# Sums of an attention kernel by DMA transpose in 116 units instead of 96, and its last unit in two halves

## The chip, the cores and the metric

The kernel runs on one core of one Trainium2 chip. A core has TensorE (PE, matrix products; its weight loads are listed as PEld), VectorE (DVE), ScalarE (ACT), GpSimd (POOL) and SyncE (SP, which here only issues transfers). Each works through its own list of instructions in order; semaphores tie the lists together. The metric is the device time of one execution in microseconds.

## The reference

B = 1, 2048 tokens, width D = 512, 32 heads of 128, 2048 cached keys, inputs in bfloat16:

```python
x = A_x
xn = _layernorm(x)
q = (xn @ wq).reshape(B, Sq, 32, 128).transpose(0, 2, 1, 3)
scores = einsum("bhqd,bhkd->bhqk", q, k_cache) * 128 ** -0.5
o = einsum("bhqk,bhkd->bhqd", softmax(scores), v_cache)
s = o.transpose(0, 2, 1, 3).reshape(B, Sq, 4096) @ wo
h = _gelu(_layernorm(xn) @ w1)                # four column groups shifted by 1, -1, 2, -2 tokens
x1 = xn + shifted(h) @ w2
g = _silu(x1 + _gelu(_layernorm(x1) @ w3) @ w4)   # w3: 512 x 1792
return x + s * g
```

## The kernel before, in words

All instructions stay in the order in which the program names them: `pin` keeps them so on each engine, and `mm` (L109) issues every matmul. The tile framework adds the semaphores.

A prologue computes the layernorms and the MLP. `m1` to `m4` are its four products, `x1` and `x2` add a product to `xall`, `stats` and `ln2` make the second layernorm. The second half of the last product (tiles 8 to 15, `m4`) is left over: `held_mm` slips it into the first units of the attention loop. `q_ahead` makes the queries of some units during the prologue.

The attention is a loop over 128 **units**: 8 groups of 4 heads, in each group 4 query blocks of 512 tokens, in each block the 4 heads. A unit has 8 **slots** (`SPU`), and `n` counts slots over all units. In a slot, `s_slot` makes the scores of 256 keys by two matmuls of 512 columns into a pair of PSUM banks (`psS`, two pairs), and ACT takes their exponentials into a quarter of `pT` (L291). `pv_run` follows `lag` slots later with `pv_slot`: two matmuls of values by exponentials into `ps_o` (`psO`, two banks). The lag is 5 at first, 10 from unit 12, and 5 again at the end.

The softmax sums take two ways. DVE always adds the four `pT` quarters to one 128 x 512 tile `acc` (L297, L302, then L307 and L308). In units outside `TURN`, `sums` multiplies this by a column of ones on TensorE: four matmuls of one column into a bank of `psX` with the tag `xa`, which the query projection `q_mm` uses as well; DVE takes the reciprocals (L327). In units inside `TURN` (12 to 107), `turn` transposes `acc` by a DMA on SP's queue (L333), and `turned_sums` sums it on DVE (L338) and takes the reciprocals (L340). Both write the reciprocals to DRAM (`dr`), and `bcast` (L346) reads them back to all partitions as `rb`. `norm` (L358) multiplies `ps_o` by `rb` into `oT`, which frees the bank of `ps_o`. In turned units the token order of `rb` differs from that of `ps_o`: `rb` is read in steps of 4 elements (16 bytes), `ps_o` and `oT` in a row.

When all four heads of a block are normalised, `wo_mm` multiplies `oT` by their rows of wo, one tile of 128 tokens after another, and `wo_post` adds the product to `sacc` (L399, L411, or L404 and L407 for late tiles). In the last group it also gates and writes out (L420, L422, or `y_out` L392). SP's queue carries, in order, the loads of K (transposed), V, wq and wo pieces of the next group, `turn`'s transposes, `dr`, `rb` and the outputs.

The last two units are called UA (126) and UB (127). UB has no round trip through DRAM for its sums: `late_sums` sums by matmuls with a column of twos, and the reciprocals scale the rows of its part of the product (`late_wo`, `last_act`, L458), which an identity matmul (`join`) adds to the part of the other three heads (`last_wo`).

Of the kernel before, what the change touches and what calls it, by code (L numbers as in the profile page):

```python
# [17 lines left out]
def kernel(  # L18
# [62 lines left out]
    ident = const.tile([P, P], BF16, name="ident")  # L81
    diag = const.tile([P, P], FP32, name="diag")
# [36 lines left out]

    units = [(g, qt, hh) for g in range(NG) for qt in range(QT) for hh in range(HG)]  # L120
# [3 lines left out]
    TURN = range(3 * HG, NU - 5 * HG)  # L124
    PV0, PV1 = 2 * HG, NU - 5 * HG + 3
# [177 lines left out]

    def add_last(u):
        add_next(u, 3)
        a = st[u]["acc"]
        pin(nc.vector.tensor_tensor(out=a[:, 0:2, :], in0=a[:, 0:2, :], in1=a[:, 2:4, :], op=ALU.add))  # L307
        pin(nc.vector.tensor_tensor(out=a[:, 0, :], in0=a[:, 0, :], in1=a[:, 1, :], op=ALU.add))  # L308
# [11 lines left out]
    def sums(u):  # L320
        s = st[u]
        ps = psX.tile([P, 4], FP32, tag="xa", name="ps_sum")
        a = s["acc"][:, 0, :].rearrange("k (p j) -> k j p", j=4)
        for j in range(4):
            mm(ps[:, j:j + 1], a[:, j, :], ones_t[:], True, True)
        rc = smp.tile([P, 4], FP32, name="rc")
        pin(nc.vector.reciprocal(out=rc[:], in_=ps[:]))  # L327
# [21 lines left out]
    def norm(u):  # L349
# [17 lines left out]
    def wo_mm(g, t, hhs):  # L367
        if hhs[0] == 0:
            wo_box[0] = psX.tile([P, D], FP32, tag="xm", name="ps_wo")
        oT = oTs[(g, t // 4)]  # L370
        ts = t % 4
        for hh in hhs:
            mm(wo_box[0][:], oT[:, hh, ts * P:(ts + 1) * P], wos[g * HG + hh][:], hh == 0, hh == HG - 1)
# [53 lines left out]
    def late_sums(u, src, first, last):  # L427
        if first:
            st[u]["sum"] = psX.tile([P, 4], FP32, tag="xa", name="ps_sum")
        ps = st[u]["sum"]  # L430
        for j in range(4):
            for i, a in enumerate(src):
                mm(ps[:, j:j + 1], a[:, j * P:(j + 1) * P], twos_t[:],
                   first and j == 0 and i == 0, last and j == 3 and i == len(src) - 1)

    def late_rc(u):
        rc = smp.tile([P, 4], FP32, tag="rl", bufs=2, name="rl")
        pin(nc.vector.reciprocal(out=rc[:], in_=st[u]["sum"][:]))
        st[u]["rc"] = rc

    def late_o(u):
        s = st[u]
        s["ou"] = pB.tile([P, 512], BF16, tag="ou", bufs=1, name="ou")
        for c in (slice(0, 256), slice(256, 512)):
            pin(nc.scalar.activation(out=s["ou"][:, c], in_=s["o"][:, c], func=ACT.Identity))

    def late_wo(u, ts, ps):
        h = units[u][0] * HG + units[u][2]
        mm(ps, st[u]["ou"][:, ts * P:(ts + 1) * P], wos[h][:], True, True)

    def last_wo(ts, ps, hhs=(0, 1, 2), stop=False):
        for hh in hhs:
            mm(ps, oTs[(NG - 1, QT - 1)][:, hh, ts * P:(ts + 1) * P], wos[(NG - 1) * HG + hh][:],
# [105 lines left out]
    for u in range(NU - 4 * HG, NU - 3 * HG):  # L559
# [8 lines left out]
    for u in (2 * HG, NU - 12, NU - 2, NU - 1):  # L568
# [60 lines left out]
    HELD = 7  # L629
    heldps = {}  # L630

    def held_part(t, a, b, tag="xm"):
        if a == 0:
            heldps[t] = psX.tile([P, 512], FP32, tag=tag, name="ps_m")
        m4(t, heldps[t], range(a, b))
# [7 lines left out]
    def held_mm(n):  # L643
        u, p = divmod(n, SPU)
        if u == 0 and p < 2:
            held_part(8, 7 * p, 7 * p + 7, "xa")
            if p == 1:
                held_out(8, n)
        elif u == 0:
            held_part(9, FC * (p - 2) // 6, FC * (p - 1) // 6)  # L650
            if p == SPU - 1:
                held_out(9, n)
        elif u < HELD:
            if p < SPU - 1:
                held_part(9 + u, 2 * p, 2 * p + 2)
            if p == SPU - 2:
                held_out(9 + u, n)
# [28 lines left out]
    def wo_slot(part, n, each=2):  # L686
        gg, t = wo_todo[0]
        if part < HG // each:
            wo_mm(gg, t, tuple(range(part * each, (part + 1) * each)))
# [7 lines left out]
    for v in range(1, NU):  # L697
        if v not in made:
            for dc in range(DC):
                k = dc - 1 if v - 2 in TURN else dc // 2  # L700
                q_plan[(v - 1) * SPU + k].append((v, (dc,)))

    for n in range(UB * SPU):
        u, p = divmod(n, SPU)
        extra = len(wo_todo) > 3 and u < 2 * HG + 2 and pS is not None or u >= UA - 1
# [14 lines left out]
        if twice and p < 3:  # L720
            wo_slot(p, n)
        if p == (3 if u - 1 in TURN else 2) and u + 1 not in made:
# [133 lines left out]
```

## Time and profile before

| | us |
|---|---|
| median of 3 runs | 1253.55 (1253.39 to 1253.73) |
| the profiled execution | 1253.59 |
| its span, first to last instruction | 1251.8 |
| PE busy | 1237.9 |
| ACT busy | 1101.5 |
| DVE busy | 1031.9 |

The granted TensorE clock was 0.999 of full speed over the span. A row of a group gives line, engine, operation, what is written from what, the count, the busy time and the mean of one in ns, and then the idle time of the engine before it with what ended it. A row of the timeline gives the start, the time, and the same names; rows that follow each other are merged (x2), and then the time is that of all together. Matmuls overlap, so the time of one is longer than the distance to the next. In a row of stretches, the busy times stand in the order PE, PEld, DVE, ACT, POOL. Idle time of an engine that does not set the end costs nothing.

### The profile page before, as it was taken

How to read it: one execution, taken by the hardware profiler on the slowest of the kernel's cores; microseconds unless marked ns; L12 is line 12 of the kernel's file. 1: busy time of each engine (PE TensorE's matmuls, PEld its weight loads, DVE VectorE, ACT ScalarE, POOL GpSimd, SP SyncE). 2: the span in 40 equal slices, each digit the busy share in tenths (PEclk: the TensorE clock that was granted, in tenths of full speed). 3: DMA queues.
4: the chain of work that ended last, by engine and by line, in shares of the span. 5: the costliest groups of instructions: out<-in, count | busy, mean ns of one | idle time of the engine just before them, and what ended most of it. 6: DMA issues, size and time to landing. Idle time of an engine off the chain costs nothing.

```text
span 1251.8 us, 16270 instructions
## 1 busy us (share of the span) xinstructions
PE 1237.9 (99%) x5814; PEld 597.8 (48%) x5931; DVE 1031.9 (82%) x1430; ACT 1101.5 (88%) x1117; POOL 35.5 (3%) x91
## 2 busy tenths in 40 slices
PE   9999999999999999999999999999999999999998
PEld 4444444444444444444444444444444444444443
DVE  7621567788888988888888888888888999978888
ACT  5344888999999999999999999999999999998886
POOL 5310000000000000000000000000000000000000
PEclk9999999999999999999999999999999999999999
DMA  6482112444244523453244514353244424442222
GB/s 180 112 161 54 18 26 43 87 106 81 53 89 93 118 52 64 97 110 77 68 83 106 103 39 93 80 119 68 57 100 102 103 66 86 99 92 50 68 56 59
DMA packets 224945, 103.86 MB, mean 83 GB/s; under 512 B 176928, under 2 KB 208160, under 8 KB 224864
## 3 DMA queue, kind: packets, MB, share of 16 engines
q1 hardware_dynamic: 223488, 100.33, 37.7%
q0 software_dynamic: 672, 1.84, 0.8%
q8 instruction: 46, 0.75, 0.3%
q10 hardware_dynamic: 704, 0.66, 0.2%
q14 instruction: 35, 0.29, 0.1%
HBM read 67.90 MB, written 2.36 MB: 56 GB/s over the span
## 4 chain that ended last, share of the span: by engine, by line
PE 96%; DVE 2%; issue 1%; ACT 1%; DMA 1%; POOL 0%; SPq 0%; DVEq 0%; ACTq 0%
PE ps_s L109 39%; PE ps_o L109 36%; PE ps_q L109 9%; PE ps_wo L109 9%; PE ps_m L109 2%; DVE acc L302 0%; DMA rb<-dr 0%; PE ps_sum L109 0%; PE ps_w L109 0%; DMA xin<-in_A_x_dram 0%; ACT qT L277 0%; DVE y L392 0%; DVE xall L420 0%; ACT pT L291 0%; DVE sacc L411 0%
## 5 line engine op out<-in xcount | busy, mean ns | idle before, releaser
L291 ACT ACTIVATE pT<-ps_s 128x1024 bf16<-128x1024 f32 x1024 | 1035.2, 1024 | 75.4 <-PE ps_s L109 27.8
L109 PE MATMUL ps_s<-qT,kT 128*128 128x512 bf16 x2041 | 607.6, 379 | 0.6
L109 PE MATMUL ps_o<-pT,vb 128*128 128x512 bf16 x1962 | 588.9, 379 | 0.5
L302 DVE TENSOR_TENSOR acc<-acc,pT 128x2048 bf16<-128x2048 bf16 x255 | 309.3, 1213 | 83.7 <-ACT pT L291 80.2
L109 PEld LDWEIGHTS <-kT 128*128 128x128 bf16 x2048 | 230.3, 113 | 226.6 <-issue 0.8
L109 PEld LDWEIGHTS <-vb 128*128 128x128 bf16 x2048 | 200.3, 98 | 226.4 <-issue 0.4
L109 PE MATMUL ps_wo<-wo_h,oT 128*128 128x512 bf16 x492 | 177.8, 379 | 2.1
L109 PE MATMUL ps_q<-xnT,wq_h 128*128 128x512 bf16 x481 | 172.9, 379 | 2.1
L297 DVE TENSOR_TENSOR acc<-pT 128x2048 bf16<-128x2048 bf16 x128 | 155.9, 1218 | 6.1 <-ACT pT L291 5.9
L358 DVE TENSOR_TENSOR oT<-ps_o,rb 128x512 bf16<-128x512 f32 x127 | 124.6, 981 | 15.8 <-DMA rb<-dr 15.3
L307 DVE TENSOR_TENSOR acc<-acc 128x1024 bf16<-128x1024 bf16 x127 | 87.9, 692 | 4.3
L275 DVE CAST qT<-ps_q 128x512 bf16<-128x512 f32 x112 | 76.5, 683 | 0.3 <-PE ps_q L109 0.3
L109 PEld LDWEIGHTS <-oT 128*128 128x128 bf16 x508 | 48.5, 98 | 56.1 <-DVE oT L358 0.7
L109 PEld LDWEIGHTS <-wq_h 128*128 128x128 bf16 x484 | 47.2, 98 | 56.1 <-issue 0.2
L411 DVE TENSOR_TENSOR sacc<-ps_wo,sacc 128x512 f32<-128x512 f32 x96 | 66.3, 691 | 3.2 <-PE ps_wo L109 2.7
L338 DVE TENSOR_REDUCE sm<-tT 128x4 f32<-128x512 bf16 x96 | 65.5, 682 | 0.5 <-DMA tT<-acc 0.4
L308 DVE TENSOR_TENSOR acc<-acc 128x512 bf16<-128x512 bf16 x127 | 54.0, 425 | 4.3
L242 ACT ACTIVATE h2T<-ps_s 128x1024 bf16<-128x1024 f32 x28 | 28.7, 1025 | 24.0 <-PE ps_s L109 24.0
L109 PE MATMUL ps_s<-xn2T,w_sb 128*128 128x512 bf16 x219 | 48.6, 379 | 0.3
L109 PEld LDWEIGHTS <-w_sb 128*128 128x128 bf16 x336 | 30.3, 98 | 32.1
L109 PEld LDWEIGHTS <-h2T 128*128 128x128 bf16 x224 | 21.5, 98 | 25.0 <-issue 0.2
L109 PE MATMUL ps_m<-w_sb,h2T 128*128 128x512 bf16 x106 | 31.0, 379 | 0.5
(75 smaller groups left out, 334.7 us busy)
## 6 DMA issues: line engine op xcount, KB each, us to landing
rb<-dr SPq DMA_DIRECT2D x127, 256.0 KB, 3.9
vb<-in_A_v_cache_dram SPq DMA_DIRECT2D x64, 256.0 KB, 3.1
wq_h<-in_A_wq_dram SPq DMA_DIRECT2D x32, 128.0 KB, 3.1
wo_h<-in_A_wo_dram SPq DMA_DIRECT2D x32, 128.0 KB, 3.1
w_sb<-in_B_w_dram SPq DMA_DIRECT2D x8, 256.0 KB, 4.9
kT<-in_A_k_cache_dram SPq DMA_TRANSPOSE x128, 3.0
xl<-in_A_x_dram SPq DMA_DIRECT2D x16, 128.0 KB, 3.6
dr<-rc SPq DMA_DIRECT2D x127, 2.0 KB, 1.4
```

The costliest lines, as they stand in the source:

```text
L109: pin(nc.tensor.matmul(out=out, lhsT=lhsT, rhs=rhs, start=start, stop=stop))
L242: pin(nc.scalar.activation(out=h2[c, f][:], in_=ps[:], func=ACT.Gelu_apprx_tanh))
L275: pin(nc.vector.tensor_copy(out=qT[:], in_=st[u].pop("psq")[:]))
L291: pin(nc.scalar.activation(out=s["pT"][-1][:, jj:jj + 2, :], in_=sps[:], func=ACT.Exp, scale=SCALE))
L297: pin(nc.vector.tensor_tensor(out=s["acc"][:], in0=s["pT"][0][:], in1=s["pT"][1][:], op=ALU.add))
L302: pin(nc.vector.tensor_tensor(out=a[:], in0=a[:], in1=st[u]["pT"][i][:], op=ALU.add))
L307: pin(nc.vector.tensor_tensor(out=a[:, 0:2, :], in0=a[:, 0:2, :], in1=a[:, 2:4, :], op=ALU.add))
L308: pin(nc.vector.tensor_tensor(out=a[:, 0, :], in0=a[:, 0, :], in1=a[:, 1, :], op=ALU.add))
L338: pin(nc.vector.tensor_reduce(out=sm[:], in_=s["tT"][:], axis=mybir.AxisListType.X, op=ALU.add))
L358: pin(nc.vector.tensor_tensor(out=to, in0=o, in1=rb, op=ALU.mult))
L411: pin(nc.vector.tensor_tensor(out=sa, in0=ps[:], in1=sa, op=ALU.add))
```

## The change

- `TURN` becomes units 0 to 115: units 0 to 11 and 108 to 115 get their sums by transpose as well. The tile `tT` moves to another pool.
- `norm` of turned units reads `rb` in a row and writes `oT` in a row; now `ps_o` is read in steps of 128 elements (512 bytes). `oT` so holds these tokens in another order, and `o_cols` picks a tile's 128 columns in steps of 4 as the weights of `wo_mm`.
- The value matmuls lag by 10 slots from the first unit, and go back to 5 over units 119 to 123 (before: 111 to 115).
- The leftover MLP product is dealt out matmul by matmul (`held`), in two banks by turns.
- The queries made ahead are those of units 0 to 8, 120 to 124 and 127 (before: 0 to 8, 112 to 116, 126 and 127).
- In units that are not turned, `norm` moves to slot 4, `sums` to slot 5, the four output matmuls to one a slot. In units 121 and 126 a second tile goes in slots 1 to 3.
- UB is done in two halves of 256 tokens: `half_slot` makes 512 keys by 256 tokens in a slot, first all keys of half 0, then of half 1, and the rest follows half by half (`half_pv`, `half_add`, `half_sums`, `half_o`, `half_wo`). UA's sums take two chunks of `acc`, so one folding addition on DVE goes.

The core of the diff (further parts that are left out rename, or follow from these):

```diff
-    TURN = range(3 * HG, NU - 5 * HG)
-    PV0, PV1 = 2 * HG, NU - 5 * HG + 3
+    TURN = range(NU - 3 * HG)
+    PV1 = NU - 3 * HG + 3
...
-    def sums(u):
+    def sums(u, chunks=1):
         s = st[u]
         ps = psX.tile([P, 4], FP32, tag="xa", name="ps_sum")
-        a = s["acc"][:, 0, :].rearrange("k (p j) -> k j p", j=4)
         for j in range(4):
-            mm(ps[:, j:j + 1], a[:, j, :], ones_t[:], True, True)
+            for i in range(chunks):
+                a = s["acc"][:, i, :].rearrange("k (p j) -> k j p", j=4)
+                mm(ps[:, j:j + 1], a[:, j, :], ones_t[:], i == j == 0, j == 3 and i == chunks - 1)
         rc = smp.tile([P, 4], FP32, name="rc")
         pin(nc.vector.reciprocal(out=rc[:], in_=ps[:]))
         s["dr"] = drp.tile([P, 4], FP32, name="dr")
         pin(nc.sync.dma_start(out=s["dr"][:], in_=rc[:]))
 
     def turn(u):
-        st[u]["tT"] = pS.tile([P, 4, P], BF16, tag="tT", bufs=2, name="tT")
+        st[u]["tT"] = pB.tile([P, 4, P], BF16, tag="tT", bufs=2, name="tT")
         pin(nc.sync.dma_start_transpose(out=st[u]["tT"][:], in_=st[u]["acc"][:, 0, :]))
 
...
         if u in TURN:
-            o, to = (x.rearrange("k (j p) -> k j p", j=4) for x in (o, to))
-            rb = rb.rearrange("k (p j) -> k j p", j=4)
+            o = o.rearrange("k (j p) -> k p j", j=4)
+            rb, to = (x.rearrange("k (p j) -> k p j", j=4) for x in (rb, to))
         pin(nc.vector.tensor_tensor(out=to, in0=o, in1=rb, op=ALU.mult))
...
+    def o_cols(g, qt, hh, ts):
+        o = oTs[(g, qt)][:, hh, :]
+        if (g * QT + qt) * HG + hh in TURN:
+            return o.rearrange("k (p j) -> k j p", j=4)[:, ts, :]
+        return o[:, ts * P:(ts + 1) * P]
+
...
+    half = ({}, {})
+
+    def half_keys(t):
+        return t[:].rearrange("p a (b c) -> p (a b) c", b=2)
+
+    def half_slot(u, i, p):
+        g, qt, hh = units[u]
+        kv = kTs[g * HG + hh].rearrange("d (i p j) -> d i j p", p=P, j=KJ)
+        sps = half_keys(psS.tile([P, 2, 512], FP32, name="ps_s"))
         for j in range(4):
-            for i, a in enumerate(src):
+            kc = 4 * p + j
+            mm(sps[:, j, :], kv[:, kc // KJ, kc % KJ, :], st[u]["qT"][:, 256 * i:256 * i + 256], True, True)
+        if p % 2 == 0:
+            half[i][p // 2] = half_keys(pB.tile([P, 4, 512], BF16, tag="pT", bufs=6, name="pT"))
+        jj = 4 * (p % 2)
+        pin(nc.scalar.activation(
+            out=half[i][p // 2][:, jj:jj + 4, :], in_=sps, func=ACT.Exp, scale=SCALE))
+
+    def half_pv(u, i, p):
+        g, qt, hh = units[u]
+        if p == 0:
+            pl, tag = ((psO, "ps_o"), (psX, "xm"))[i]
+            half[i]["o"] = pl.tile([P, 256], FP32, tag=tag, name="ps_oh")
+        for j in range(4):
+            kc = 4 * p + j
+            mm(half[i]["o"][:], vBs[g * HG + hh][:, kc, :], half[i][p // 2][:, 4 * (p % 2) + j, :],
+               kc == 0, kc == KC - 1)
+
...
-    for u in (2 * HG, NU - 12, NU - 2, NU - 1):
+    for u in (2 * HG, NU - 1, NU - HG):
...
+        for _ in range((4, 10)[n] if n < 2 else 3 if n < 2 * LAG else 2 if n % SPU < 5 else 1):
+            if not held:
+                return
+            t, fc = held.popleft()
+            if fc == 0:
+                heldps[t] = psX.tile([P, 512], FP32, tag=("xa", "xm")[t % 2], name="ps_m")
+            m4(t, heldps[t], (fc,))
+            if fc == FC - 1:
+                held_out(t, n)
...
-        if u < PV0:
-            lag = LAG
-        elif u < PV0 + LAG:
-            lag = LAG + u - PV0 + 1
-        elif u < PV1:
+        if u < PV1:
...
-                k = dc - 1 if v - 2 in TURN else dc // 2
+                k = dc - 1 if v - 2 >= TURN.start else dc // 2
...
-        late = 0 if u <= NU - 5 * HG else 2 if u <= NU - 5 * HG + 2 else 1
-        if p == (7 if u - 2 in TURN else 2 + late) and 2 <= u:
+        if u - 2 < TURN.start:
+            norm_p, sum_p, wo_p, each = 2, 3, 4, 2
+        elif u - 2 in TURN:
+            norm_p, sum_p, wo_p, each = 7, 5, 3, 1
+        else:
+            norm_p, sum_p, wo_p, each = 4, 5, 4, 1
+        if p == norm_p and 2 <= u and not u - 2 in TURN:
             norm_queue(u - 2)
-        if p == 3 + late and 1 <= u and u - 1 not in TURN:
+        if p == sum_p and 1 <= u and u - 1 not in TURN:
             sums(u - 1)
-        if p == 4 + late and 1 <= u and u - 1 not in TURN:
+        if p == sum_p + 1 and 1 <= u and u - 1 not in TURN:
             bcast(u - 1)
-        each, p0 = (1, 3) if u - 2 in TURN else (2, 4)
-        if p0 <= p <= p0 + HG // each and wo_todo and pS is not None:
-            wo_slot(p - p0, n, each=each)
+        if u in (NU - 7, UA) and p in (1, 2, 3):
+            wo_slot(p - 1, n)
+        if wo_p <= p <= wo_p + HG // each and wo_todo and pS is not None:
+            wo_slot(p - wo_p, n, each=each)
+        if p == norm_p and u - 2 in TURN:
+            norm_queue(u - 2)
...
+        half_slot(UB, p // 4, p % 4)
+        if p < LAG:
+            pv_run(n + p)
+        else:
+            half_pv(UB, 0, p - LAG)
         if p == 0:
+            wo_slot(4, n, each=1)
+            add_next(UA, 3)
+            fold(UA)
+        if p in (1, 2, 3):
+            wo_slot(p - 1, n + p)
+        if p == 2:
+            sums(UA, 2)
         if p == 3:
             norm(UB - 2)
         if p == 4:
             bcast(UA)
+            half_add(0, half[0][0], half[0][1][:, 0:4, :])
+        if p == 5:
+            half_add(0, half[0][0], half[0][1][:, 4:8, :], slice(4, 8))
         if p == 6:
...
+    half_pv(UB, 0, SPU - LAG)
+    half_o(0)
+    half_pv(UB, 1, 0)
+    half_sums(0, [half[0]["acc"][:, k, :] for k in range(4)])
+    half_add(1, None, half[1][1][:, 0:4, :])
+    half_pv(UB, 1, 1)
+    for ts in (0, 1):
+        half_wo(UB, ts, wl[ts])
+        scaled(ts)
+    for ts in (0, 1):
+        last_wo(ts, ps[ts], (0, 1))
+    half_pv(UB, 1, 2)
+    norm(UA)
+    half_add(1, None, half[1][1][:, 4:8, :])
+    half_add(1, None, acc[:, 2:4, :], slice(0, 2))
+    for ts in (0, 1):
+        last_wo(ts, ps[ts], (2,))
+    join(0)
+    half_sums(1, [acc[:, k, :] for k in range(2)])
+    half_pv(UB, 1, 3)
+    half_o(1)
     join(1)
+    last_gate(t0, tb[0])
+    wl[2] = bank(psX, "xm")
+    wl[3] = bank(psX, "xa")
+    for ts in (2, 3):
+        half_wo(UB, ts, wl[ts])
+        scaled(ts)
+    for ts in (2, 3):
+        ps[ts] = bank(psO, "ps_o")
+        last_wo(ts, ps[ts])
+        mm(ps[ts], ident2[:], tb[ts][:], False, True)
+    tb[2] = last_act(ps[2], 0.5)
+    for ts in (0, 1, 2):
+        if ts:
+            last_gate(t0 + ts, tb[ts])
+        y_out(t0 + ts, tb[ts], (nc.sync, nc.scalar)[ts % 2])
+    tm = pS.tile([P, D], FP32, tag="tm", bufs=4, name="tm")
+    pin(nc.vector.scalar_tensor_tensor(
+        out=tm[:], in0=ps[3], scalar=0.5, in1=xall[:, t0 + 3, :], op0=ALU.mult, op1=ALU.mult))
+    y_out(t0 + 3, tm, nc.scalar)
```

More of the change, by code (lines that the diff above doesn't have):

```diff
@@ new lines, in half_pv, with half_add @@
+    def half_pv(u, i, p):
[7 more added lines that the diff above has]
+               kc == 0, kc == KC - 1)
+    def half_add(i, a, b, cols=slice(0, 4)):
+        if "acc" not in half[i]:
+            half[i]["acc"] = half_keys(pB.tile([P, 4, 512], BF16, tag="acc", bufs=2, name="acc"))
+        a = half[i]["acc"] if a is None else a
+        pin(nc.vector.tensor_tensor(out=half[i]["acc"][:, cols, :], in0=a[:, cols, :], in1=b, op=ALU.add))
@@ new lines, in half_sums, with half_o @@
+    def half_sums(i, src):
+        ps = psX.tile([P, 2], FP32, tag="xa", name="ps_sum")
+        for k, a in enumerate(src):
+            for j in range(2):
+                mm(ps[:, j:j + 1], a[:, j * P:(j + 1) * P], twos_t[:],
+                   k == j == 0, k == len(src) - 1 and j == 1)
+        rc = smp.tile([P, 2], FP32, tag="rl", bufs=2, name="rl")
+        pin(nc.vector.reciprocal(out=rc[:], in_=ps[:]))
+        half[i]["rc"] = rc
+    def half_o(i):
+        half[i]["ou"] = pB.tile([P, 256], BF16, tag="ou", bufs=2, name="ou")
+        pin(nc.scalar.activation(out=half[i]["ou"][:], in_=half[i]["o"][:], func=ACT.Identity))
@@ L558 @@
         stats(xall[:, t, :], mv2, rs2, t)
-    for u in range(NU - 4 * HG, NU - 3 * HG):
+    for u in range(NU - 2 * HG, NU - HG):
         q_ahead(u)
@@ L627 @@
             at((b - 4 - hh // 2) * SPU + (5, 7)[hh % 2], lambda h=h: load_wo(h))
-    HELD = 7
     heldps = {}
[L632 to L635, printed above, removed]
+    held = deque((t, fc) for t in range(8, NT) for fc in range(FC))
     def held_out(t, n):
@@ L704 @@
         u, p = divmod(n, SPU)
[L705 removed]
+        extra = len(wo_todo) > 3 and u < 2 * HG + 2 and pS is not None
+        if p == 0 and wo_box:
+            wo_slot(4, n, each=1)
         s_slot(u, p)
@@ L740 @@
             fn()
-        if n == HELD * SPU - 1:
+        if pS is None and not held:
             right.close()
```

121 lines of the change are left out of this document (28 added, 93 removed).

## The prediction

> **What bounds the kernel now.** I read the page first, then the chain, then single tiles and stretches of the timeline. The change in three parts: 20 more units get their softmax sums by a DMA transpose instead of TensorE; one projection moves from the prologue into the loop; the last unit is cut in two.
>
> ```profile
> span 1251.8 us, 16270 instructions
> PE 1237.9 (99%) x5814; PEld 597.8 (48%) x5931; DVE 1031.9 (82%) x1430; ACT 1101.5 (88%) x1117; POOL 35.5 (3%) x91
> PE 96%; DVE 2%; issue 1%; ACT 1%; DMA 1%; POOL 0%; SPq 0%; DVEq 0%; ACTq 0%
> L109 PEld LDWEIGHTS <-kT 128*128 128x128 bf16 x2048 | 230.3, 113 | 226.6 <-issue 0.8
> L109 PEld LDWEIGHTS <-vb 128*128 128x128 bf16 x2048 | 200.3, 98 | 226.4 <-issue 0.4
> ```
>
> TensorE is busy 99% of the span and carries 96% of the chain: the time is the length of its stream. So the change is worth what it takes out of that stream, plus or minus the waits at both ends. The matmuls are pipelined, so I need their spacing and not their 379 ns.
>
> ```profile
> 1238.37 2.75 PE L109 MATMUL ps_o<-pT,vb 128*128 128x512 bf16 x12
> 1234.76 0.59 PE L109 MATMUL ps_o<-pT,vb 128*128 128x512 bf16 x2
> 1235.19 0.27 PE L109 MATMUL ps_sum<-ones_t,acc 128*128 128x1 bf16 x4
> 1235.32 0.38 PE L109 MATMUL ps_s<-qT,kT 128*128 128x512 bf16 x1
> 1241.02 0.35 PE L109 MATMUL ps_sum<-twos_t,acc 128*128 128x1 bf16 x8
> 1241.24 0.34 PE L109 MATMUL ps_sum<-twos_t,pT 128*128 128x1 bf16 x8
> ```
>
> Twelve in a row take 2.75 us, less one's 0.379: 11 steps of 215.5 ns. A set of four sum matmuls pushes the next score matmul from 1235.19 to 1235.32, 0.13 us; the sixteen of the last unit start 27.5 ns apart (0.22 us for eight), which would make 0.11 us a set.
>
> What a unit with sums costs in all is read from the spacing of one instruction per unit: the reciprocals L327 where TensorE sums, the query copies L275 where the sums are transposed.
>
> ```profile
> L327 DVE RECIPROCAL rc<-ps_sum x10: 169/178/183, 149.2 to 233.0; 128x4 f32<-128x4 f32 x10
> L327 DVE RECIPROCAL rc<-ps_sum x19: 172/182/183, 1081.2 to 1235.5; 128x4 f32<-128x4 f32 x19
> L275 DVE CAST qT<-ps_q x88: 681/683/684, 284.5 to 1036.4; 128x512 bf16<-128x512 f32 x88
> ```
>
> By the program's order 380 matmuls of 512 columns stand between the first and the last of the ten: 81.9 us by the step. The row says 83.8, so 1.9 us over 9 sets, 0.21 each. Between the nineteen stand 700, 150.9 us of 154.3: 3.4 over 18 sets, 0.19 each. The transposed units hold 40 each, 8.62 us; the row gives 751.9/87 = 8.64, 0.02 over. So a set costs 0.17 to 0.19 us more than a transposed unit, not 0.11: the waits of PE and DVE on the one bank that the query and the sums share count too.
>
> **The change part by part.** *Sums of units 0 to 11 and 108 to 115.* 20 sets leave the stream: 12 x 0.19 + 8 x 0.17 = 3.65 us. In their place each unit gets a reduction on DVE and a transpose on SP.
>
> ```profile
> L338 DVE TENSOR_REDUCE sm<-tT x96: 665/685/686, 254.3 to 1075.8; 128x4 f32<-128x512 bf16 x96
> DMA to landing us min/median/max: 2.4/3.7/5.3
> 623.99 1.23 DVE L302 TENSOR_TENSOR acc<-acc,pT 128x2048 bf16<-128x2048 bf16 x1 [0.93 <-ACT pT L291]
> 625.14 1.08 DVE L358 TENSOR_TENSOR oT<-ps_o,rb 128x512 bf16<-128x512 f32 x1
> 1226.22 0.69 DVE L392 TENSOR_TENSOR y<-tm,sacc 128x512 bf16<-128x512 f32 x1
> 1226.83 0.68 DVE L358 TENSOR_TENSOR oT<-ps_o,rb 128x512 bf16<-128x512 f32 x1
> 126.00:204.00 78.00, 77.44 (x378) 37.81 (x385) 51.56 (x68) 67.17 (x72) 0.00 (x0) 1.00 0.12 24
> 1049.00:1066.00 17.00, 16.89 (x78) 8.21 (x79) 16.08 (x23) 16.11 (x17) 0.00 (x0) 1.00 0.44 93
> 1092.00:1126.00 34.00, 33.84 (x168) 16.60 (x170) 27.54 (x37) 31.03 (x33) 0.00 (x0) 1.00 0.49 94
> 300.00:900.00 600.00, 597.05 (x2726) 288.47 (x2780) 528.84 (x695) 569.00 (x557) 0.00 (x0) 1.00 0.40 82
> ```
>
> The transposes land after 3.7 us (2.4 to 5.3), issued five slots of some 1.1 us before their reduction, so SP's queue, K pieces behind it included, keeps its rhythm from the 96 units that have this already. DVE (third busy figure of a stretch) is the cover to watch. In units 0 to 8 it has 26 of 78 us free; the additions are 0.68 for the reduction and at most 0.40 for the normalisation: under 8 us. In the middle 71 of 600 us are free, 1.03 a unit. In units 106 to 107, 16.08 of 17 us are busy, 0.46 a unit free. In units 111 to 114, 6.8 of 8.4; there come the reduction and a query copy that was made ahead before, 0.61 each (an operation overlaps the one before it by 0.08: 1226.22 to 1226.83), and 0.40: 8.4 of 8.63. Full, but not over. So the reductions cost the span nothing; where their cover goes, each costs what it overruns.
>
> *The normalisation, reciprocals in a row (norm).* Plain it takes 0.68 us (unit 124, 1226.83), with rb read in steps of 16 bytes 1.08. After, rb is in a row, but ps_o is read in steps of 512 bytes. No row shows a stepped read of ps_o; ends: 0.68 (steps free) and, by the 0.40 that rb's steps cost taken twice or three times, 1.5 or 1.9. I take 1.08, the row nearest to it, one stepped operand. Effect on the sum: zero, as DVE has the room above; at 0.68 zero too. The weights read from oT now have steps of 4 elements; kT's have them already, 113 against 98 ns a load, and the stream's step is the same in score and value matmuls (1234.76 to 1235.19 is two steps). Zero.
>
> *The held MLP matmuls and lag 10 from the start.* The 112 matmuls and all value matmuls stay, only in other slots; two banks alternate. Zero, at most one 0.6 us tanh uncovered on ACT.
>
> *One projection less ahead.* Units 112 to 116 and 126 were made ahead, now 120 to 124: four matmuls, 0.86 us, enter the loop. In the prologue they go, but not with their whole length:
>
> ```profile
> 46.22 4.64 PE L109 MATMUL ps_o<-w_sb,hT 128*128 128x512 bf16 x20
> 46.68 0.18 DVE L181 BATCH_NORM_AGGREGATE mv<-bn 128x2 f32<-128x6 f32 x1
> 47.29 0.69 DVE L225 TENSOR_TENSOR xall<-ps_o,xall 128x512 bf16<-128x512 f32 x1 [0.43 <-PE ps_o L109]
> ```
>
> The twenty m2 matmuls would start 0.86 earlier, but their first result waits for DVE's statistics, done at 46.86, before L225 can free the bank that the third result needs. L225 gains 0.43 idle at most, so the prologue gains some 0.35: net +0.5 us.
>
> *Late units (117 to 126).* Eleven sets remain; the four output matmuls (wo) of a tile go over four slots instead of two, with a second tile in units 121 and 126; their number stays.
>
> ```profile
> 1218.80 0.61 DVE oT L358
> 1219.46 0.59 PE ps_o L109 x2
> L302 DVE TENSOR_TENSOR acc<-acc,pT 128x2048 bf16<-128x2048 bf16 x255 | 309.3, 1213 | 83.7 <-ACT pT L291 80.2
> L307 DVE TENSOR_TENSOR acc<-acc 128x1024 bf16<-128x1024 bf16 x127 | 87.9, 692 | 4.3
> L308 DVE TENSOR_TENSOR acc<-acc 128x512 bf16<-128x512 bf16 x127 | 54.0, 425 | 4.3
> L411 DVE TENSOR_TENSOR sacc<-ps_wo,sacc 128x512 f32<-128x512 f32 x96 | 66.3, 691 | 3.2 <-PE ps_wo L109 2.7
> ```
>
> The first two rows, of the chain, are the one wait for ps_o's bank in the late units of before: norm behind a full DVE queue in unit 125, which has two tiles. That one may go. But norm moves from slot 3 to slot 4, while the values of units 123 to 126 start at slot 5. Ahead of it stand an output step (0.69, twice, and 0.42 of the same kind as L308), three additions (1.21, 0.69, 0.43) and a query copy (0.68); with norm 5.5 us at most, while TensorE reaches slot 5's values 5 x 1.08 + 0.43 = 5.8 us into the unit. So no wait, or one of up to an estimated 0.25 where DVE starts late. I take zero for the stage.
>
> *The last unit.* Rows of its end:
>
> ```profile
> 7.20 0.89 PE ps_m L109 x16
> 1241.46 0.69 DVE L358 TENSOR_TENSOR oT<-ps_o,rb 128x512 bf16<-128x512 f32 x1 [0.49 <-DMA rb<-dr]
> 1242.21 0.39 PE L109 MATMUL ps_w<-wo_h,oT 128*128 128x512 bf16 x1 [0.18 <-DVE oT L358]
> 1246.23 0.38 PE L109 MATMUL ps_w<-tb,ident 128*128 128x512 bf16 x1 [0.40 <-ACT tb L458]
> 1248.22 0.69 DVE L392 TENSOR_TENSOR y<-tb,sacc 128x512 bf16<-128x512 bf16 x1
> ```
>
> Sixteen 128-column matmuls take 0.89, 55.6 ns each; between that and 215.5 a 256-column one is 109 ns. 64 of them in place of 32: +0.07; one identity matmul more: +0.22; the sums 20 to 20. From 1238.37 to 1246.23 are 7.86 us; the stream between them (12 value, 16 output and 2 identity matmuls, 16 sums) is 30 x 0.2155 + 16 x 0.0275 = 6.90, so 0.96 are waits (the 0.18 and 0.40 of these rows among them). They mostly go, since half 1's value matmuls fill the time in which oT and tb are awaited: -0.8. But UA's folded sums now wait for DVE (+0.15), and at the very end DVE does y, a 0.69 gating and y for the last two tiles one after the other, where before ACT took a share: from tile 2's tb to the last y some 0.42 + 3 x 0.65, 0.3 to 0.5 more. Together 0, between -0.6 and +0.7.
>
> **Sum.** -3.65 + 0.5 + 0 + 0 = -3.15, so about -3.2 us. The profiled execution took 1253.59 (span 1251.8 and 1.8 around it), the median of the runs is 1253.55: the same within 0.04. Forecast 1253.59 - 3.2 = **1250.4 us**; its own range is 1249.3 to 1251.2 (a set at 0.25 or at 0.14, the end from -0.6 to +0.7).
>
> **The rivals.** *A: only array time goes (chance 0.12).* If the 0.17 to 0.19 are not of the sums but of the loop's order, 20 sets are worth 20 x 0.11 = 2.2, less 0.5: 1251.9. For it: the step of 27.5 ns. Against: the transposed units have no overrun at all. [...]
>
> *B: waits in units 123 to 126 and at the end come out at their bounds (0.06).* 4 x 0.25 + 0.7 of the 3.2 are lost: 1251.9 to 1252.1. For it: the order in DVE's queue. Against: the wait now shown is one in ten units.
>
> *C: slower (0.12): the stepped read of ps_o is far dearer than rb's.* It decides from a norm of some 1.7 us. At 1.87 (three times 0.40) DVE overruns in units 111 to 117 by 0.55 each and in the 16 before them, 95 to 110, taken as full as 106 and 107, by 0.33: 7 x 0.55 + 16 x 0.33 = 9 us: 1259. At 2.26 the middle overruns also, and it is over 1275. At 1.47 only 1 us is lost. For it: each element then lies 512 bytes from the next, against 16 for rb. Against: nothing in rb's 0.40 says that distance counts. [...]
>
> *D: the norm does not get shorter at all.* It is what I reckoned with (1.08), about as likely as not; it moves the time by nothing, so it is no case of its own.
>
> **How the numbers follow.** A measurement of this kernel tells about 0.2%, 2.5 us, from no change: faster is below 1251.05. Forecast 0.70, A 0.12, B 0.06, C 0.12. Faster gets the forecast's 0.70 and the better end of A and B, 0.02; same 0.16; slower C. The range 1249.2 to 1252.4 holds the forecast, A and B, and leaves out C and some of the lower tail.
>
> **What would show it.** Right: periods of 8.63 from unit 9 to 116, no L327 before unit 117; L358 at 1.08 or less; PE still 99%. Wrong: DVE without idle time in 1049 to 1126, L358 over 1.5, PE waiting for DVE in units 111 to 126, or a wait at the m2 matmuls over 0.6.

## The result, and the profile after

The changed kernel takes 1250.28 us (median of 9 runs, 1249.84 to 1250.99) beside 1253.54 us of the kernel before (9 runs, 1253.32 to 1254.05): ratio 0.9974, interval 0.9965 to 0.9982. Forecast were 1250.4. Run again later, on the chip of e9 to e11, it took 1251.23 beside 1254.19, ratio 0.9977 (0.9969 to 0.9986). The profiled execution took 1249.84 and was the fastest of the nine, so the traces differ by more (3.75 us) than the medians (3.26).

The page, the rows that answer to those of before:

```profile
span 1248.0 us, 16327 instructions
PE 1241.3 (99%) x5884; PEld 606.2 (49%) x5884; DVE 1007.5 (81%) x1452; ACT 1111.2 (89%) x1117; POOL 35.4 (3%) x91
PE 99%; DVE 1%; ACT 1%; issue 0%; ACTq 0%
L365 DVE TENSOR_TENSOR oT<-ps_o,rb 128x512 bf16<-128x512 f32 x127 | 86.7, 682 | 10.1 <-DMA rb<-dr 10.0
L345 DVE TENSOR_REDUCE sm<-tT 128x4 f32<-128x512 bf16 x116 | 78.6, 678 | 1.2 <-DMA tT<-acc 0.9
L110 PEld LDWEIGHTS <-oT 128*128 128x128 bf16 x508 | 56.7, 112 | 58.6 <-issue 0.2
```

The span is 3.8 us shorter and the chain is now TensorE nearly throughout. norm (L365) takes 682 ns in the mean over all units, where a plain one of the kernel before took 0.68 us: the strided read of ps_o costs nothing here. The strided weights cost 112 ns a load (98 in the kernel before), hidden under the matmuls, as the turned units below keep their 40 steps of 215.5 ns.

The rhythm, from the rows of single lines (the first for 260 to 1145 us), and all that TensorE waited for by the view of waits:

```profile
L345 DVE TENSOR_REDUCE sm<-tT x103: 674/676/687, 262.8 to 1142.4; 128x4 f32<-128x512 bf16 x103
L334 DVE RECIPROCAL rc<-ps_sum x11: 175/182/183, 1147.4 to 1231.3; 128x4 f32<-128x4 f32 x11
PE ps_warm L110 <- DVE nhalf L115: 1.2, 1, 1.2
PE ps_w L110 <- ACT ou L485: 0.3, 1, 0.3
PE ps_o L110 <- DVE xall L227: 0.3, 1, 0.3
```

879.6/102 makes 8.62 us a turned unit; TensorE sums only 11 times before the last unit, from unit 117 on; in the loop it waits for nobody in this trace. VectorE's cover in the stretches of the prediction:

```profile
1049.00:1066.00 17.00, 17.00 (x81) 8.29 (x80) 15.25 (x23) 16.12 (x17) 0.00 (x0) 1.00 0.48 117
1092.00:1126.00 34.00, 34.00 (x160) 16.59 (x158) 31.53 (x46) 32.30 (x32) 0.00 (x0) 1.00 0.66 120
```

15.25 of 17 us where it was 16.08, and 31.53 of 34 where 27.54: 2.47 us free over four units. Rows of the end:

```profile
1239.28 0.38 PE L110 MATMUL ps_w<-tb,ident 128*128 128x512 bf16 x1
1240.67 0.61 PE L110 MATMUL ps_w<-wo_h,ou 128*128 128x512 bf16 x2 [0.26 <-ACT ou L485]
1244.68 0.69 DVE L404 TENSOR_TENSOR y<-tm,sacc 128x512 bf16<-128x512 f32 x1
```

Where the 3.8 us lie, read from the first exponential of each unit: prologue -0.47, units 0 to 12 -2.21 (120.50 to 118.29), units 13 to 107 0.00 (820.17 in both), units 108 to 126 -1.02 (165.15 to 164.13), and from there to the end -0.08 (20.19 to 20.11).

### The profile page after: what moved, and what is told of

It is laid out like the page before. It is cut to its first block, busy times and chain, and to the rows that moved or that the text cites. A ratio compares the mean times of both kernels' runs of the same rounds, so it can differ in the third digit from the quotient of the medians.

```text
span 1248.0 us, 16327 instructions
## 1 busy us (share of the span) xinstructions
PE 1241.3 (99%) x5884; PEld 606.2 (49%) x5884; DVE 1007.5 (81%) x1452; ACT 1111.2 (89%) x1117; POOL 35.4 (3%) x91
## 4 chain that ended last, share of the span: by engine, by line
PE 99%; DVE 1%; ACT 1%; issue 0%; ACTq 0%
PE ps_s L110 40%; PE ps_o L110 38%; PE ps_wo L110 9%; PE ps_q L110 8%; PE ps_m L110 2%; PE ps_warm L110 0%; PE ps_oh L110 0%; ACT qT L279 0%; DVE bn L182 0%; ACT tb L501 0%; ACT xnT L201 0%; PE ps_w L110 0%; PE ps_sum L110 0%; DVE y L404 0%; DVE xall L227 0%
## 5 line engine op out<-in xcount | busy, mean ns | idle before, releaser
L110 PE MATMUL ps_s<-qT,kT 128*128 128x512 bf16 (+1 forms) x2064 | 609.1, 377 | 0.0
L110 PE MATMUL ps_o<-pT,vb 128*128 128x512 bf16 x2032 | 603.5, 379 | 0.0
L110 PEld LDWEIGHTS <-kT 128*128 128x128 bf16 x2064 | 232.9, 113 | 218.0
L110 PE MATMUL ps_wo<-wo_h,oT 128*128 128x512 bf16 x496 | 186.7, 379 | 0.0
L299 DVE TENSOR_TENSOR acc<-pT 128x2048 bf16<-128x2048 bf16 x127 | 155.3, 1223 | 36.0 <-ACT pT L293 35.6
L110 PE MATMUL ps_q<-xnT,wq_h 128*128 128x512 bf16 x488 | 180.1, 379 | 0.0
L365 DVE TENSOR_TENSOR oT<-ps_o,rb 128x512 bf16<-128x512 f32 x127 | 86.7, 682 | 10.1 <-DMA rb<-dr 10.0
L110 PEld LDWEIGHTS <-oT 128*128 128x128 bf16 x508 | 56.7, 112 | 58.6 <-issue 0.2
L345 DVE TENSOR_REDUCE sm<-tT 128x4 f32<-128x512 bf16 x116 | 78.6, 678 | 1.2 <-DMA tT<-acc 0.9
```

Of the source, the lines that this page charges most:

```text
L110: pin(nc.tensor.matmul(out=out, lhsT=lhsT, rhs=rhs, start=start, stop=stop))
L299: pin(nc.vector.tensor_tensor(out=s["acc"][:], in0=s["pT"][0][:], in1=s["pT"][1][:], op=ALU.add))
L345: pin(nc.vector.tensor_reduce(out=sm[:], in_=s["tT"][:], axis=mybir.AxisListType.X, op=ALU.add))
L365: pin(nc.vector.tensor_tensor(out=to, in0=o, in1=rb, op=ALU.mult))
```

## The experiments

Below, a **stall** of a unit is what its period, from first exponential to first exponential, has over 8.63 us in the profiled execution; it changes from run to run. "before" is the kernel before on the same chip. e1 to e4 ran on one chip, e5 to e8 on another, e9 to e11 and the second run of the changed kernel on a third.

| kernel | median us | before | ratio (interval) | stalls in units 13 to 116 |
|---|---|---|---|---|
| changed | 1250.28 | 1253.54 | 0.9974 (0.9965 to 0.9982) | 0 |
| changed, again | 1251.23 | 1254.19 | 0.9977 (0.9969 to 0.9986) | 1.7 |
| e1 rb in steps | 1253.54 | 1253.86 | 0.9996 (0.9987 to 1.0005) | 4.0 |
| e2 early sums on TensorE, one bank | 1256.11 | 1253.86 | 1.0017 (1.0008 to 1.0026) | 0 |
| e3 late sums on TensorE | 1252.14 | 1253.86 | 0.9987 (0.9979 to 0.9996) | 0.6 + the sums |
| e4 one query more ahead | 1250.75 | 1253.86 | 0.9975 (0.9964 to 0.9985) | 0.9 |
| e5 e1, norm first | 1261.22 | 1254.26 | 1.0054 (1.0041 to 1.0067) | 7.2 |
| e6 norm first | 1253.33 | 1254.26 | 0.9992 (0.9984 to 1.0001) | 1.2 |
| e7 old end | 1253.14 | 1254.26 | 0.9990 (0.9981 to 0.9999) | 1.7 |
| e8 one bank | 1256.26 | 1254.26 | 1.0016 (1.0007 to 1.0025) | 1.2 |
| e9 e1, shifted | 1250.16 | 1254.19 | 0.9968 (0.9956 to 0.9981) | 0.4 |
| e10 changed, shifted | 1249.98 | 1254.19 | 0.9965 (0.9953 to 0.9978) | 0 |
| e11 before, shifted | 1254.88 | 1254.19 | 1.0008 (0.9999 to 1.0017) | 0.5 + the sums |

### Does the shorter norm matter? e1

```diff
-            o = o.rearrange("k (j p) -> k p j", j=4)
-            rb, to = (x.rearrange("k (p j) -> k p j", j=4) for x in (rb, to))
+            o, to = (x.rearrange("k (j p) -> k j p", j=4) for x in (o, to))
+            rb = rb.rearrange("k (p j) -> k j p", j=4)
...
-        if (g * QT + qt) * HG + hh in TURN:
-            return o.rearrange("k (p j) -> k j p", j=4)[:, ts, :]
         return o[:, ts * P:(ts + 1) * P]
```

> Changed kernel, but norm of turned units reads rb in steps of 16 bytes again and ps_o in a row, and oT keeps the token order of ps_o. My theory: norm goes from 0.68 back to 1.08 us, DVE still has room in every turned unit (fullest: units 111 to 117, about 8.25 of 8.63 us), so unit periods stay 8.63 and the time stays within 0.3 us of the changed kernel (about 1250.3). Rival, DVE is the cover that the change needs: units 111 to 117 overrun by 0.1 to 0.4 each, the time is 0.7 to 3 us longer.

Measured: 1253.54, nearly all of the gain lost. The theory fell, and with it the zero that the prediction gave the norm at either length. The loss is not spread over the units. Seven units (15, 31, 47, 63, 79, 95, 111, one in each head group) are 0.3 to 1.1 us longer; all others keep 8.63. The timeline of unit 15, in e1 and then in the changed kernel:

```profile
262.97 1.05 DVE L365 TENSOR_TENSOR oT<-ps_o,rb 128x512 bf16<-128x512 f32 x1 [2.31 <-DMA rb<-dr]
264.07 0.59 PE L110 MATMUL ps_o<-pT,vb 128*128 128x512 bf16 x2 [0.94 <-DVE oT L365]
...
262.06 0.69 DVE L365 TENSOR_TENSOR oT<-ps_o,rb 128x512 bf16<-128x512 f32 x1 [1.51 <-DMA rb<-dr]
262.86 0.59 PE L110 MATMUL ps_o<-pT,vb 128*128 128x512 bf16 x2
```

In the changed kernel norm frees the bank at 262.75 and the values take it at 262.86: 0.1 us to spare. In e1 norm starts 0.9 later, because rb came later (0.1 of it because the whole loop starts later), and ends 1.3 later. Both wait for rb; in e1 it lands later.

### Is it VectorE's order? e5, e6

The change had also put norm behind the output step of slot 7. First theory: that took the slack, and the shorter norm gave it back. e5 is e1, e6 the changed kernel, with norm ahead again:

```diff
+        if p == norm_p and u - 2 in TURN:
+            norm_queue(u - 2)
         if u in (NU - 7, UA) and p in (1, 2, 3):
...
-        if p == norm_p and u - 2 in TURN:
-            norm_queue(u - 2)
```

> The normalisation reads the reciprocals in steps of 16 bytes again (1.08 us), and stands on VectorE ahead of the output step of slot 7 again, as in the kernel before; everything else is the changed kernel. Theory (the long normalisation cost 3.3 us only because the change also put it 0.6 us later on VectorE, and TensorE's next value matmul of the same bank came 0.1 us after the shortened one): the normalisation ends at about 8.67 us into an ordinary unit, as in the kernel before, and the stalls of units 15, 31, 47, 63, 79, 95 and 111 go from 4.0 us in sum to 0.5 or less; 1250.3 to 1250.9. Rival (its length costs by itself, through VectorE's load or the ring of sums behind it): the stalls stay at 2 us or more and the time at 1252.3 to 1253.5.

> The changed kernel with the normalisation ahead of the output step of slot 7 on VectorE. Theory: it ends at about 8.27 us into an ordinary unit instead of 8.88, the wait for VectorE in units 15, 31 and so on never reaches TensorE, and as the changed kernel shows almost no such stall in its profile the gain is 0 to 0.4 us: 1249.9 to 1250.3. Rival (the output step, now 0.69 us later, holds up the bank of the output matmuls): a stall at slot 0 or 3 of every unit, 1251 or more.

Both fell, with the opposite sign: e5 is the worst of all kernels, e6 loses most of the gain. In the seven units the time is set by a chain: dr, rb behind it, norm behind rb, and then TensorE, which wants the bank 1.9 us into the unit. What norm's end has over that is the stall: in unit 15 norm ends 1.85 us into the unit in the changed kernel, 2.06 in e6, 2.68 in e5 and 3.01 in e1, and the stalls are 0, 0.15, 0.77 and 1.10. In the kernel before it ends at 1.18.

VectorE's order does not set the start of this chain. dr is issued 3.1 to 3.2 us into unit 14 in all five, though the reduction starts at 0.2 us in the changed kernel, 0.6 in e1 and e6 and 1.8 in e5. So the longer norm costs its own length here, 0.4 us, and the rest is when rb lands. In e6 rb takes 3.4 to 3.7 us to land in the seven units, in the changed kernel 3.2 to 3.4; why was not traced.

Behind a stall the chain can close to a loop: a late norm puts off the reduction of the next unit, that one its dr and rb, and these the next norm. e5 shows it: units 111 to 116 start their reductions at 3.3 to 3.7 us, where the changed kernel has 0.9 to 1.5, and all six stall, by 0.2 to 0.6. Part of e5's and e6's loss, 3.3 and 1.0 us, is in unit 117, where TensorE waits for the query copy (1.2 and 0.9) and in e5 for norm (1.7).

### What delays rb: the loads of TensorE's instructions. e9, e10, e11

What differs between before and after is how long dr takes to land in the unit ahead of the stalled one. The DMA view of unit 14 (first before, then e1; KB and median us to landing at the end of a row):

```profile
kT<-in_A_k_cache_dram SPq DMA_TRANSPOSE x1, 2.8
dr<-rc SPq DMA_DIRECT2D x1, 2.0 KB, 1.8
...
q8 instruction: 1, 0.02, 1.7%
kT<-in_A_k_cache_dram SPq DMA_TRANSPOSE x1, 4.4
dr<-rc SPq DMA_DIRECT2D x1, 2.0 KB, 3.3
```

dr is issued at the same place in both (3.2 us into the unit, behind the same V and K pieces), but it lands after 3.3 us instead of 1.8, and a packet of 16 KB of kind "instruction" is there. In these units of all groups dr takes 1.7 to 2.6 us in the kernel before (units 14 to 94; its unit 110 is not turned) and 3.0 to 3.5 in the changed kernel and e1 (units 14 to 110). The page of the changed kernel has the whole queue:

```profile
q8 instruction: 46, 0.75, 0.3%
```

46 packets of 16 KB for some 11,770 instructions of TensorE: one load for every 256 in the mean. In units 14, 30, 46 and so on of the changed kernel each takes 0.9 to 1.1 us, and a part of K and dr waits. The single packets of the trace show how: in unit 14 of the changed kernel 120 of dr's 128 packets start 4.19 to 4.38 us into the unit; the load lasts from 4.24 to 5.17, and the last 8, a sixteenth, start at 5.18 to 5.25. The page counts 16 DMA engines; the trace names a packet's queue and not its engine, so that one of the 16 held the load and these 8 is my reading. A turned unit has 80 instructions (40 matmuls, 40 weight loads), a head group 1280, and behind the load in unit 14 the trace has 30 more up to the one in unit 110, five a group: so each group meets them in nearly the same place. In the changed kernel that is 3.4 to 4.2 us into units 14, 30, 46 and so on, just under dr; in the kernel before it was 1.0 to 1.6 us into units 13, 29 and 45, long before dr. The change moved the loads because it took instructions out of TensorE's list: 8 for each of 12 sets and 8 of a query, 104 in all, are 1.3 units, and the loads come 1.3 units later.

The profile does not say whose code q8 carries. That it is TensorE's follows from the count and from the loads' moves with TensorE's list, by 1.3 units here and by some 3.4 us in the test below. None of TensorE's three waits in the changed kernel (1.2, 0.3 and 0.3 us) is for code: what the load holds up there is the data behind it, as the packets show.

The test leaves the loop alone and only moves the loads: e9 is e1, e10 the changed kernel, e11 the kernel before, with other dummy matmuls at the very start, as many columns in all but 32 instructions more (e11: 60).

```diff
-    warm_mm(11)
+    for _ in range(27):      # e11: 41 of 137 columns
+        mm(wps[:, 0:208], warm[:, 0:P], warm[:, 0:208], True, True)
```

> The kernel of e1_rb_steps (reciprocals read in steps, normalisation 1.08 us), with one edit more: the 11 dummy matmuls of 512 columns at the very start are 27 of 208 columns, the same columns in all, so that TensorE's stream holds 32 instructions more ahead of everything else. Theory (the stalls of units 15, 31, 47 and so on come from the load of TensorE's next 256 instructions, 16 KB and about 1 us of one DMA engine, which falls at 3.4 to 4.2 us into units 14, 30, 46 and so on, where the write of the reciprocals waits behind it): the loads fall some 3.4 us earlier, at 0 to 0.8 us, the write lands after 1.4 to 2.6 us instead of 3.1 to 3.5, and the stalls go from 4.0 us in sum to 1 or less: 1250.3 to 1251.3. Rival (the stalls follow from the length of the normalisation alone, or from the pieces of K and V): nothing changes, 1253.2 to 1254.2.

> The changed kernel with the same 27 dummy matmuls of 208 columns in place of 11 of 512. Theory: its own rest of such stalls (none to 1.5 us, from run to run and chip to chip) goes, so 0.2 to 1.2 us less than the changed kernel beside it, and a narrower spread of times. Rival: no difference, or the loads fall on another transfer that is waited for and new stalls appear in other units.

> The kernel before, with 41 dummy matmuls of 137 columns in place of 11 of 512: 60 instructions more ahead of TensorE's stream, and nothing else. Theory: the loads that fell at 3.0 to 4.9 us into units 16, 32, 48 and so on fall some 6.5 us earlier, at 5.2 to 7.0 us into units 15, 31, 47, on the broadcast that the normalisation of that unit waits for; that has 0.0 to 0.6 us of room before TensorE needs its bank, so each head group gets a stall of up to 1 us: 2 to 6 us in sum, 1256 to 1260. Rival (these loads do not hold up data): as before, within 0.3 us.

> The changed kernel itself, as the measure for the three others on the same chip. From the first result 1250.3; with stalls in units 15, 63, 79 and 111 as other runs of its order showed, up to 1251.9.

e9 takes 1250.16 (ratio 0.9968 on its chip, where e1 had 0.9996 on its own): the long norm costs nearly nothing any more, one stall of 0.4 in unit 15. The loads stand at 0.0 to 0.4 us into the units, or just ahead of them, and dr takes 1.7 to 2.1 us; in unit 14 all its 128 packets start together, at 4.20 to 4.53. Unit 14 of e9 by the DMA view, then TensorE's waits for norm in e1, in e9 and in the changed kernel's second run (sum, times, longest):

```profile
kT<-in_A_k_cache_dram SPq DMA_TRANSPOSE x1, 3.0
dr<-rc SPq DMA_DIRECT2D x1, 2.0 KB, 2.1
...
PE ps_o L110 <- DVE oT L365: 2.5, 5, 0.9
PE ps_o L110 <- DVE oT L365: 0.2, 1, 0.2
PE ps_o L110 <- DVE oT L365: 1.2, 3, 0.5
```

e10 takes 1249.98 (1249.78 to 1250.05) beside 1251.23 (1250.64 to 1252.9) of the changed kernel: 1.25 us less, a spread of 0.3 instead of 2.3, and no stall. It beats both kernels by changing dummy matmuls alone. The one cause that e1, e9, e10 and the packets leave standing is the place of the loads. e2 says the same unasked: its 12 sets of sums put 96 instructions into TensorE's list, dr takes 1.7 to 2.1 us in it, and it has no stall; e8, the same without the sums, has 1.2 us of them.

One thing more is open. Unit 15 stalls longest in e1 and in the second run of the changed kernel, 1.1 and 0.7 us, and rb takes 4.0 and 3.9 us to land there. A packet of a second queue of kind "instruction" (q14) lies under rb for 1.8 us in both, and for 0.55 in the first run of the changed kernel, where rb takes 3.3. Whether it delays rb was not tested.

e11 is the weak half. Expected were 2 to 6 us; measured were 0.7, with an interval that holds no change. Its runs spread from 1254.45 to 1256.61 (before: 1253.73 to 1254.88), and the profiled one, 1254.48, is among the shortest, so its trace cannot show what the longest hold. In it the loads came 5.3 to 7.8 us into units 15 to 95 (expected: 5.2 to 7.0), and by the waits of one line norm waited longer for rb (before, then e11):

```profile
  DMA rb<-dr: 15.3, 20
  DMA rb<-dr: 23.4, 38
```

but only units 16 and 96 show a stall that the kernel before has not, 0.24 each. These two follow the latest loads, at 7.8 us into units 15 and 95, where rb takes 5.9 and 5.6 us to land instead of 3.9 and 4.3. In units 15, 31 and so on norm ends at 1.0 to 1.7 us, before TensorE wants the bank at 1.9: the kernel before had more room under rb than I gave it.

### What a set of sums costs: e2, e8, e3

```diff
-    TURN = range(NU - 3 * HG)
+    TURN = range(3 * HG, NU - 3 * HG)          # e2;  e3: range(NU - 5 * HG)
...
-                heldps[t] = psX.tile([P, 512], FP32, tag=("xa", "xm")[t % 2], name="ps_m")
+                heldps[t] = psX.tile([P, 512], FP32, tag="xm", name="ps_m")   # e2, e8
...
-            wo_slot(p, n, tag="xa")
+            wo_slot(p, n)                                                      # e2, e8
```

> Changed kernel, but units 0 to 11 get their sums by matmuls again (the leftover MLP product then stays in one bank, and the output product of unit 7 too). My theory, a set costs the stream 0.17 to 0.19 us net: 2.0 to 2.3 us longer than the changed kernel, about 1252.5. Rival A, only the array time goes (0.11 a set): 1.3 us longer, 1251.6. Rival, the early gain came from the lag or the two banks: less than 0.5 us.

> The changed kernel with the held MLP matmuls and the early output matmuls all in one PSUM bank; the sums of units 0 to 11 stay transposed. Theory (of the 6 us that the early sums on TensorE cost in one bank, 2.2 are the sums and the rest comes from the one bank, where a tile's first matmul waits for VectorE to read the tile before): 1253.0 to 1254.5. Rival (the sums alone did it, each tile of the bank is read in time): 1250.3 to 1250.8.

> Changed kernel, but units 108 to 115 get their sums by matmuls again, the lag of the changed kernel kept. My theory, 0.17 net a set: 1.4 us longer than the changed kernel, periods of units 109 to 116 at 8.80 instead of 8.63, about 1251.7. Rival A: 8 x 0.11 = 0.9 us longer, periods of 8.74.

e2 lost 6 us where 2 were expected; e8, which has the single bank without the sums, loses nearly as much. (One of e2's eleven runs took 2682.13 us, which was not explained; the median does not rest on it.) The additions L299 of units 0 to 12, within 117 to 252 us, e2 and then e8, those of units 8 to 12 alone, within 205 to 250 us, and a wait of e8:

```profile
L299 DVE TENSOR_TENSOR acc<-pT x13: 1215/1224/1227, 130.0 to 245.3; 128x2048 bf16<-128x2048 bf16 x13
L299 DVE TENSOR_TENSOR acc<-pT x13: 1215/1226/1226, 129.9 to 243.9; 128x2048 bf16<-128x2048 bf16 x13
L299 DVE TENSOR_TENSOR acc<-pT x5: 1224/1224/1226, 210.1 to 245.3; 128x2048 bf16<-128x2048 bf16 x5
L299 DVE TENSOR_TENSOR acc<-pT x5: 1226/1226/1226, 209.4 to 243.9; 128x2048 bf16<-128x2048 bf16 x5
PE ps_m L110 <- DVE xall L253: 3.6, 4, 1.9
```

Over the twelve sets e2 is 1.3 us longer than e8, 0.11 us a set. But a set costs more where nothing hides it: in units 8 to 12, behind the left-over product, four periods take 35.2 us in e2 and 34.5 in e8, 8.80 against 8.63, 0.17 a set. In the units before, the waits for the single bank take up a part (unit 7 has 8.94 us in e2 and 9.18 in e8). The single bank costs 4.65 us by the first exponential of unit 13 (248.28 instead of 243.63): 3.6 us of that are the waits of the last row, for VectorE to read the product before. That is the price of one bank under the new dealing of this product; the kernel before has no such wait, though its tiles 9 to 15 go through one bank. In e3 seven periods between the query copies of units 109 to 116 (e3, then the changed kernel, 1080 to 1150 us) give 61.7 against 60.6:

```profile
L277 DVE CAST qT<-ps_q x8: 683/683/685, 1084.7 to 1146.4; 128x512 bf16<-128x512 f32 x8
L277 DVE CAST qT<-ps_q x8: 683/684/684, 1084.9 to 1145.5; 128x512 bf16<-128x512 f32 x8
```

0.16 a set by these rows, which are rounded to 0.1 us; most of these units have 8.77 us instead of 8.63, and from the first exponential of unit 108 to that of 127 e3 takes 1.09 us more for its eight sets: 0.14. The rest of what the trace of e3 is longer, 0.6 us, are stalls of the kind above, in units 15, 63 and 79.

### The query made ahead: e4

```diff
-    for u in (2 * HG, NU - 1, NU - HG):
+    for u in (2 * HG, NU - 1, NU - HG, NU - 2):
```

> Changed kernel, with the query of unit 126 made in the prologue as before the change. My theory: four matmuls (0.86 us) leave unit 125, the prologue grows by only 0.35 to 0.5, since they stand where TensorE waits for DVE; the time is 0.4 to 0.5 us shorter, about 1249.8. Rival, the moved matmuls cost the same in both places: no difference (within 0.1 us in the traces).

1250.75, no gain. The prologue grew by 0.79 us (first exponential at 126.13 instead of 125.34), units 124 and 125 shrank by 0.21 and 0.60. Four matmuls cost the same in both places; the rest of the difference of its trace is stalls in units 15, 63 and 111.

### The halves of the last unit: e7

The parts `half_*` and the end of the program are those of the kernel before, `late_sums`, `late_wo` and so on; UA's sums are folded fully again. The core:

```diff
-        half_slot(UB, p // 4, p % 4)
-        if p < LAG:
-            pv_run(n + p)
-        else:
-            half_pv(UB, 0, p - LAG)
+        s_slot(UB, p)
+        pv_run(n + p)
...
-            add_next(UA, 3)
-            fold(UA)
+            add_last(UA)
```

> The changed kernel with the last unit whole, as in the kernel before (the sums of unit 126 folded fully, one set of four; no halves). Prediction: the halving is worth 0, between -0.6 and +0.7, so 1249.6 to 1250.9; from the two profiles (20.19 against 20.07 us from the first exponential of unit 127 to the end) 0.1 us, so about 1250.4. Rival (the halving saves the 0.96 us of waits and the old end loses more, as one more output tile now lies in it): 1251 or more.

The rival was right: from the first exponential of unit 127 to the end it takes 21.23 us instead of 20.11 (and 20.19 in the kernel before). One row of e7 has it:

```profile
1241.45 0.39 PE L110 MATMUL ps_w<-wo_h,oT 128*128 128x512 bf16 x1 [1.28 <-DVE oT L365]
```

The old end behind the new loop waits 1.28 us for UA's norm; in the kernel before it was 0.18. What its trace is longer beside that, 1.7 us, are stalls in units 15, 47, 63, 79 and 111. Its runs also have 1.9 to 2.9 us outside the span, where the kernel before on that chip has 1.7 to 1.9; this is not explained.

## Why the prediction was right, step by step

The time came out within 0.2 us, and the main mechanism, sums taken out of TensorE's stream, is right. That the number is so close is in part luck: some terms were too large, others too small, and one zero held only because another guess was wrong.

**The sums.** Forecast 3.65 us for 20 sets, 2.28 early and 1.36 late. Early, the units 0 to 12 gained 2.21. Late, units 108 to 126 gained 1.02 with one query more in them, which e4 prices at 0.81, so 1.83 without it. The total holds, its label does not. Put back alone, eight late sets cost 1.09 (e3), and the twelve early ones 1.3, or 2.0 at the 0.17 that a set costs where nothing hides it (e2 against e8). So the 20 sets are worth 2.4 to 3.1 us, 0.12 to 0.16 each: the step that put all of the spacing, 0.17 to 0.19, on the sums gave them too much, and rival A, with 0.11, too little. A's time did not come because 0.9 to 1.6 us more came from terms that I had set at zero. 0.23 of that is in unit 125 (see below). The lag, the new slots and the new dealing of the left-over product are candidates for the rest; how it splits is not shown. e8 shows that the new dealing needs its two banks, not that they gained anything over the kernel before.

**The normalisation.** Its length came out at the lower end, 0.68, and rival C, the dear strided read, is gone. The step "Effect on the sum: zero, as DVE has the room above" failed: the forecast took 1.08, and with a norm of 1.08 the kernel is at 1253.54 (e1), above the forecast's own range. It was luck that the norm came out shorter. I had argued from VectorE's free time per unit. What counts is the chain from dr through rb to norm, once in a head group, where a load of TensorE's code lay on it. With the load moved (e9 against e10) the two lengths differ by 0.2 us: zero holds there, or nearly. Rival D, which was to move nothing, would have cost the gain.

**The query.** +0.5 was forecast, 0.86 in the loop less 0.35; the prologue gave 0.47. By e4 it is nothing at all, 0.81 in the loop against 0.79 in the prologue: the trade is even, and the 0.35 was too small. That the prologue gave only 0.47 means that some 0.3 us came into it from elsewhere. These were not traced; the profiles of kernels with the changed loop and the same queries differ by 0.2 there.

**Late units.** Zero, with a wait of up to 0.25 in units 123 to 126. No row shows TensorE waiting for oT there, so no wait was added. But one went: in the kernel before unit 125 took 9.03 us and its neighbour 124, with as many matmuls, 8.80. This 0.23 fits the wait for ps_o's bank that the prediction said may go and then left out of the sum.

**The end.** Zero between -0.6 and +0.7 was forecast, -0.08 came. But the halves hold 1.1 us against the old end in this loop (e7): two larger terms that offset each other, not two small ones. The other one, by the row of e7, is the wait for UA's norm, 1.28 us where it was 0.18; what in the new loop makes that norm later was not taken apart.

The sum: -0.47 - 2.21 - 1.02 - 0.08 = -3.78 of the 3.8 us between the two traces. The medians differ by 3.26, and 3.2 were forecast: the profiled execution of the changed kernel had no stall, its second one had 1.7 us of them, and the prediction has no term for stalls.

## What to carry to other kernels

Free time of an engine per unit does not tell what a longer instruction costs; follow the chain that it stands in, transfers included, to the place in the period where that chain has least to spare. Here 104 instructions fewer on TensorE's unrolled list moved its code loads by 1.3 units and had dr land 1.5 us later in unit 14 (3.3 us instead of 1.8). So if a stall comes back once per outer period after such a change, look for the packets of kind "instruction" in the DMA view and try the same kernel with a few more instructions at its start. A difference in spacing between two stretches prices everything that differs between them, so put a single part back before you give it the whole, and look whether another wait hides it there.

## What the runs showed of the hardware that I had not expected

- The loads of code under dr take 0.9 to 1.1 us each in the changed kernel, and in e1 a 2 KB write that met one landed after 3.3 us instead of 1.8. In the changed kernel the last 8 of its 128 packets start right behind the load. Moving the loads by 32 instructions (some 3.4 us) was worth 3.4 us in one kernel (e1 against e9, on two chips) and 1.25 in another (on one).
- The norm that reads ps_o, in PSUM, in steps of 512 bytes took 682 ns in the mean in the changed kernel, against 0.68 us for one that reads all in a row (unit 124 of the kernel before); with rb, in SBUF, read in steps of 16 bytes it took 1.08 there. For VectorE's read of this one operand the steps show no cost.
